# Starting each weight tile and each wide result tile at its own place modulo 128 bytes

## The chip, the core and the metric

The kernel runs on one core of a Trainium2 chip. The metric is the device time of one execution in microseconds; the median of three runs is compared. The profile comes from one more execution, taken by the hardware profiler.

## What is computed

The kernel does a linear recurrence with a complex decay over 768 steps for 4 x 8 heads of 48, and then a layer of 8 experts with two chosen per token. The change touches the experts alone:

```python
    logits = x @ w_gate
    noise_scale = np.log1p(np.exp(x @ w_noise))
    noisy_logits = logits + noise_scale * noise
    top2 = np.argpartition(-noisy_logits, 2, axis=1)[:, :2]
...
    for e in range(E):
        for k in range(2):
            mask = top2[:, k] == e
            h = np.maximum(x[mask] @ w1[e], 0.0)
            out[mask] += top2_w[mask, k, None] * (h @ w2[e])
```

Here E = 8, w1 is 384 x 1024 and w2 1024 x 384 for each expert, top2_w is a softmax over the two chosen, all is fp32 and there are 3072 tokens.

## The kernel before

**Stages.** In the first 260 us or so the recurrence runs in chunks of 128 steps; its gates, the choice of experts and the sending of rows to per-expert slots in DRAM run along with it, and the first weights are loaded. From there on the experts are worked one after the other. The order on each engine is written out by hand in two tables (EMIT and ORDER), and the change leaves both alone.

**An expert's slots.** Expert e (by rank) has a narrow part (w = 0) of 256 + REST[e] slots, with REST = 64, 64, 64, 48, 32, 16, 16, 0, and a wide part (w = 1) of 512 slots. So the narrow widths are 320, 320, 320, 304, 288, 272, 272 and 256.

**Split operands.** Each fp32 operand is kept as a rounded high part and a low rest. For the weights these are two tiles (`split`: a cast on ScalarE, ACT, and a subtraction on VectorE, DVE), named w1h and w1l for each of three blocks kk of 128 rows and two sets in turn (`w1{x}{kk}{e % 2}`), w2h and w2l for each of four. For x and h the high and the low part lie side by side in one tile.

**First products** (`mm1`, L896). For each of 8 blocks f of 128 columns, 9 matmuls accumulate into one PSUM tile `ph`: for kk = 0, 1, 2 the pairs (w1h, x high), (w1h, x low), (w1l, x high). A block of w1, 128 x 128, is the stationary operand (loaded by LDWEIGHTS), and x, 128 x width, moves. ACT writes the high part of h with a ReLU (L898), VectorE the low part (L901), into the tile `h{w}{f}`.

**Second products** (`mm2`, L922). For each tile j of 128 slots, 24 matmuls accumulate: for each f the pairs (h high, w2h), (h high, w2l), (h low, w2h). Here h is the stationary operand, 128 columns of it, and w2, 128 x 384, moves. The last slots of the narrow part, fewer than 128, take another form (L927, L930).

**Where tiles lie.** `mt` takes a tile from the pool that is open when its name is first used, and a pool places its tiles one behind the other in SBUF. Before the change the small tiles `spare`, `space0` and `space1`, which nothing reads, set the start: every tile of w1, w2, x and h starts 64 bytes past a multiple of 128 in each partition. A matmul's block starts a multiple of 512 bytes into its w1 tile, and so does a block of the high part of h. The low part of a wide h starts 2048 bytes into its tile, so it keeps the 64 bytes too. The low part of a narrow h starts behind the high part and its padding: for experts 3, 5 and 6 that is on a multiple of 128, for the others it is 64 past one.

Of the kernel before, what the change touches and what calls it, by code (L numbers as in the profile page):

```python
# [9 lines left out]
F32 = mybir.dt.float32  # L10
# [309 lines left out]
def kernel(  # L320
# [19 lines left out]
    ROW = 400  # L340
# [29 lines left out]
    cp = ctx.enter_context(tc.tile_pool(name="cp", bufs=1))  # L370
# [40 lines left out]
    nc.gpsimd.memset(none, 0.0)  # L411
    nc.gpsimd.memset(none[:, RNO:RNO + 1], float(NONE))
    xga = cp.tile([128, 3, ROW], F32, name="xga")
    cp.tile([128, ROW - 64], F32, name="spare")
    nc.gpsimd.memset(xga, 0.0)
    car = cp.tile([128, HD], F32, name="car")
    ncnt = small[:, 4:6]
# [329 lines left out]
    def rank():  # L747
        n = E - 2
        t = mt([128, 128], F32, name="order")
        key, place, which = t[:, 0:E], t[:, 8:8 + n], t[:, 16:16 + n].bitcast(I32)  # L750
        big, ONE[0] = (t[:, i:i + n * n].rearrange("p (r e) -> p r e", r=n) for i in (24, 64))
        ONE[2] = t[:, 100:100 + 4 * n].rearrange("p (j e) -> p j e", e=n)
        nc.vector.scalar_tensor_tensor(key, iota8, -(N + 1.0 / E), base_run, op0=OP.mult, op1=OP.add)
        nc.vector.tensor_tensor(big, key[:, None, 2:E].to_broadcast([128, n, n]),
                                key[:, 2:E, None].to_broadcast([128, n, n]), op=OP.is_gt)
        nc.vector.tensor_reduce(place, big, axis=AX.X, op=OP.add)
        nc.vector.tensor_tensor(ONE[0], iota8[:, 0:n, None].to_broadcast([128, n, n]),
                                place[:, None, :].to_broadcast([128, n, n]), op=OP.is_equal)
        nc.vector.tensor_mul(big, ONE[0], iota8[:, None, 2:E].to_broadcast([128, n, n]))
        with nc.allow_low_precision("whole numbers"):  # L760
            nc.vector.tensor_reduce(which, big, axis=AX.X, op=OP.add)
        ONE[1] = which
# [5 lines left out]
    def of(a, e):  # L768
        return a[e] if e < 2 else a[bass.ds(EX[e], 1)].rearrange("o a b -> (o a) b")
# [19 lines left out]
    def x_P(e, w):  # L789
        js = JS[w]  # L790
        src_t = (xga, xgb)[w]
        t = mt([128, len(js), 2, DM], U16, name=f"xp{w}")
        for i in range(len(js)):
            nc.scalar.copy(t[:, i], src_t[:, i, 0:DM].bitcast(U16).rearrange("p (d two) -> p two d", two=2))
        nc.sync.dma_start(xp[e % 2, js[0] * 128:(js[-1] + 1) * 128].rearrange("(j p) r -> p j r", p=128),
                          t.rearrange("p j two d -> p j (two d)"))

    def x_L(e, w):
        lo, n = JS[w][0] * 128, width(e, w)
        for kk in range(KD):  # L800
            x = XU[w, kk] = mt([128, 2, width(0, w)], U16, name=f"xu{w}", bufs=KD)[:, :, 0:n]
            for i in range(2):
                nc.sync.dma_start(x[:, i, :], xp[e % 2, lo:lo + n, i * DM + kk * 128:i * DM + (kk + 1) * 128], transpose=True)

    mctx = ctx.enter_context(ExitStack())
    mpools, psB = [], []
# [4 lines left out]

    W1, W2, XW, HT, GW, OX = {}, {}, {}, {}, {}, {}
    where = {}

    def mt(shape, dt, name, **kw):

        return where.setdefault(name, mpools[-1]).tile(shape, dt, name=name, **kw)

    def ps_tile(name, bufs=2):
        if psB:  # L820
# [7 lines left out]
    def split(raw_t, hi, lo):  # L828
        nc.scalar.copy(hi, raw_t)  # L829
        nc.vector.tensor_tensor(lo, raw_t, hi.bitcast(F32), op=OP.subtract)  # L830

    def load_w1(e):
        if e == 0:
            mt([128, 48], F32, name="space0")
        for kk in range(KD):
            r = mt([128, FF], F32, name="raw", bufs=RAW)
            nc.sync.dma_start(r, of(w1, e)[kk * 128:(kk + 1) * 128, :])
            W1[e, kk] = [mt([128, FF], F32R, name=f"w1{x}{kk}{e % 2}") for x in "hl"]
            split(r, *W1[e, kk])

    def load_w2(e):
        for f2 in range(KF // 2):
            r = mt([128, FF], F32, name="raw", bufs=RAW)
            rv = r[:, :2 * DM].rearrange("p (f d) -> p f d", f=2)
            nc.sync.dma_start(rv, of(w2, e)[f2 * 256:(f2 + 1) * 256, :].rearrange("(f p) d -> p f d", p=128))
            W2[f2] = [mt([128, 2, DM], F32R, name=f"w2{x}{f2}") for x in "hl"]
            split(rv, *W2[f2])
# [100 lines left out]
    for g in range(NG):  # L948
        f = B * g + .5
# [11 lines left out]
        for j in range(B):  # L961
            n = B * g + j
# [55 lines left out]

    at(NT - B + .5 - P["p3"] + 3 * P["d3"] + .01, close_f)
    at(P["w1"] + .5, load_w1, 0)  # L1020
    at(NT - .5 - P["q"] + .01, close_q)
    at(P["xt"] + .5, x_G, 0, 0)
# [3 lines left out]
    at(P["xt"] + .51, load_x, 1, 0, xga)  # L1026
    at(P["xu1"] + .5, x_G, 1, 0)
    at(P["w1b"] + .5, load_w1, 1)
    at(P["w2"] + .5, load_w2, 0)
    for f in range(KF):  # L1030
# [89 lines left out]
    halves(mm1, 0, 1, then)  # L1120
    then(load_x, 1, 1, xgb)
    then(load_w1, 2)
    halves(mm2, 0, 1, then)
    x_in(1, 1, then)
# [263 lines left out]
```

## Time and profile before

| | |
|---|---|
| median of three runs | 677.25 us (675.72 to 677.81) |
| profiled execution, its own time | 679.66 us |
| profiled execution, first to last instruction | 677.9 us |
| PE (matmuls) busy | 656.7 us |
| VectorE, ScalarE busy | 434.5 us, 357.6 us |
| chain that ended last: L896, L922 | 29% and 28% of the span |

PE is TensorE's matmuls and PEld its weight loads, which overlap them. A matmul's duration in the rows is longer than the distance between two starts, since matmuls are pipelined; the distance is what adds up.

### The profile page before, as it was taken

How to read it: one execution, taken by the hardware profiler on the slowest of the kernel's cores; microseconds unless marked ns; L12 is line 12 of the kernel's file. 1: busy time of each engine (PE TensorE's matmuls, PEld its weight loads, DVE VectorE, ACT ScalarE, POOL GpSimd, SP SyncE). 2: the span in 40 equal slices, each digit the busy share in tenths (PEclk: the TensorE clock that was granted, in tenths of full speed). 3: DMA queues.
4: the chain of work that ended last, by engine and by line, in shares of the span. 5: the costliest groups of instructions: out<-in, count | busy, mean ns of one | idle time of the engine just before them, and what ended most of it. 6: DMA issues, size and time to landing. Idle time of an engine off the chain costs nothing.

```text
span 677.9 us, 14399 instructions
## 1 busy us (share of the span) xinstructions
PE 656.7 (97%) x5519; PEld 578.1 (85%) x5519; DVE 434.5 (64%) x998; ACT 357.6 (53%) x596; POOL 173.3 (26%) x209
## 2 busy tenths in 40 slices
PE   7999999999989999999999999999999999999995
PEld 3477787878878899899998999999899899899895
DVE  7999999999978667444456367248337437527311
ACT  7899999999755552344226227118217406404300
POOL 3000000344443331033324124124231422422211
PEclk9999999999999999999999999999999999999998
DMA  6757667758487635256718447827636646842201
GB/s 239 232 177 193 195 156 247 219 179 273 148 244 263 216 116 203 73 174 181 220 65 299 130 140 278 149 105 272 159 122 243 164 134 218 194 127 72 63 36 35
DMA packets 100220, 117.85 MB, mean 174 GB/s; under 512 B 57338, under 2 KB 79307, under 8 KB 100144
## 3 DMA queue, kind: packets, MB, share of 16 engines
q1 hardware_dynamic: 90816, 89.32, 43.7%
q0 software_dynamic: 9328, 27.54, 12.7%
q8 instruction: 45, 0.74, 0.4%
q14 instruction: 31, 0.25, 0.1%
HBM read 70.26 MB, written 40.02 MB: 163 GB/s over the span
## 4 chain that ended last, share of the span: by engine, by line
PE 76%; DVE 8%; ACT 3%; DMA 2%; issue 1%; another core or an unknown queue 1%; SPq 0%; POOL 0%; POOLq 0%
PE ph L896 29%; PE po L922 28%; PE ptr L577 3%; PE psc L587 2%; PE pY L636 2%; PE pY L638 2%; PE psc L896 2%; PE po L930 1%; PE po L927 1%; PE cum L646 1%; DVE am L588 1%; PE cum L554 1%; DMA out_dram<-none 1%; DVE w1l L830 1%; PE cum L527 1%
## 5 line engine op out<-in xcount | busy, mean ns | idle before, releaser
L922 PE MATMUL po<-w2h,h 128*128 128x384 f32 x768 | 198.6, 335 | 0.0
L896 PE MATMUL ph<-x,w1h 128*128 128x512 f32 (+5 forms) x720 | 186.6, 347 | 0.0
L922 PEld LDWEIGHTS po<-w2h,h 128*128 128x128 f32 x768 | 139.0, 188 | 1.0 <-DVE h L901 0.3
L896 PEld LDWEIGHTS ph<-x,w1h 128*128 128x128 f32 x720 | 125.6, 188 | 15.1 <-DVE x L881 0.4
L922 PE MATMUL po<-w2l,h 128*128 128x384 f32 x384 | 128.4, 334 | 0.0
L896 PE MATMUL ph<-x,w1l 128*128 128x512 f32 (+5 forms) x360 | 124.8, 347 | 0.2 <-DVE w1l L830 0.2
L901 DVE SCALAR_TENSOR_TENSOR h<-ph,h 128x512 fp32r<-128x512 f32 (+5 forms) x168 | 71.1, 456 | 80.1 <-ACT h L898 72.5
L936 POOL DMA_INDIRECT out_dram<-ao,ox x55 | 58.1, 1056 | 247.8 <-DVE ao L935 210.5
L898 ACT ACTIVATE h<-ph 128x512 fp32r<-128x512 f32 (+5 forms) x120 | 61.1, 515 | 98.7 <-PE ph L896 85.3
L711 POOL DMA_INDIRECT xs<-xr,sl x48 | 52.8, 1100 | 186.2 <-DVE im L506 119.7
L935 DVE SCALAR_TENSOR_TENSOR ao<-po,gw,ao 128x384 f32<-128x384 f32 (+4 forms) x55 | 33.7, 613 | 78.3 <-PE po L922 77.2
L896 PEld LDWEIGHTS ph<-x,w1l 128*128 128x128 f32 x360 | 67.7, 188 | 8.1 <-DVE w1l L830 0.5
L922 PEld LDWEIGHTS po<-w2l,h 128*128 128x128 f32 x384 | 72.1, 188 | 0.4
L907 POOL DMA_INDIRECT ao<-out_dram,ox x48 | 53.3, 1111 | 51.7 <-issue 41.2
L880 ACT CAST x<-xj 128x512 fp32r<-128x512 f32 (+5 forms) x36 | 18.9, 524 | 63.6 <-DVE xj L877 63.6
L587 PEld LDWEIGHTS psc<-qT,kT 112*64 112x64 f32 x768 | 36.4, 137 | 6.7 <-issue 2.8
L587 PE MATMUL psc<-qT,kT 112*64 112x128 f32 (+1 forms) x768 | 40.2, 250 | 1.7 <-DVE h L901 1.4
L638 PE MATMUL pY<-am,v 128*48 128x128 f32 x384 | 36.4, 273 | 0.7 <-issue 0.4
L830 DVE TENSOR_TENSOR w2l<-raw,w2h 128x768 fp32r<-128x768 f32 x32 | 30.2, 953 | 8.1 <-ACT w2h L829 8.0
L588 DVE TENSOR_TENSOR am<-psc,mask 128x512 f32<-128x512 f32 x48 | 32.6, 684 | 3.6 <-PE psc L587 2.9
L829 ACT CAST w2h<-raw 128x768 fp32r<-128x768 f32 x32 | 26.3, 834 | 15.2 <-PE po L922 8.7
L636 PE MATMUL pY<-qT,z 112*48 112x128 f32 x320 | 31.8, 275 | 0.0
(229 smaller groups left out, 998.7 us busy)
## 6 DMA issues: line engine op xcount, KB each, us to landing
raw<-in_moe_w_dram SPq DMA_DIRECT2D x24, 512.0 KB
raw<-in_moe_w_dram SPq DMA_DIRECT2D x32, 384.0 KB
qk<-in_qk_dram SPq DMA_DIRECT2D x24, 384.0 KB
v<-in_v_dram SPq DMA_DIRECT2D x24, 288.0 KB
xgb<-xs SPq DMA_DIRECT2D x8, 800.0 KB
re<-in_a_dram SPq DMA_DIRECT2D x12, 384.0 KB
im<-in_a_dram SPq DMA_DIRECT2D x12, 384.0 KB
out_dram<-none SPq DMA_DIRECT2D x12, 384.0 KB
```

Of the source, the lines that this page charges most:

```text
L587: nc.tensor.matmul(p[o:o + 64, j, z:], KT[n][:, h, z:z + 64], QT[n][:, h, z:], start=True, stop=True, skip_group_check=True)
L588: nc.vector.tensor_mul(AM[n][:, 4 * half:4 * half + 4, :].rearrange("p (a r) t -> p a (r t)", r=2), p.rearrange("p (a r) t -> p a (r t)", ...
L636: nc.tensor.matmul(o, Z[b][:, h, :], QT[n][:, h, :], start=True, stop=False, skip_group_check=True)
L638: nc.tensor.matmul(o, V[n][:, H + h // 2 if h % 2 else h, :], AM[n][:, h, :], start=not g, stop=True, skip_group_check=True)
L711: d = nc.gpsimd.indirect_dma_start(out=xs, out_offset=bass.IndirectOffsetOnAxis(ap=sl[:, kk, b:b + 1], axis=0), in_=XR[g][:, lo + b, :], i ...
L830: nc.vector.tensor_tensor(lo, raw_t, hi.bitcast(F32), op=OP.subtract)
L896: nc.tensor.matmul(p[:, :n], W1[e, kk][i][:, f * 128:(f + 1) * 128], XW[w, kk][:, j, :], start=(c == 0), stop=(c == len(ms) - 1))
L898: nc.scalar.activation(h[:, 0:n], p[:, :n], AF.Relu)
L901: nc.vector.scalar_tensor_tensor(h[:, dst:dst + b - a], p[:, a:b], 0.0, h[:, a:b].bitcast(F32), op0=OP.max, op1=OP.subtract)
L907: nc.gpsimd.indirect_dma_start(out=ao[j][0:w, :], out_offset=None, in_=out, in_offset=bass.IndirectOffsetOnAxis(ap=OX[e][0:w, j:j + 1], ax ...
L922: nc.tensor.matmul(p[:, :DM], HT[w, f][i][:, o:o + 128], W2[f // 2][k2][:, f % 2, :], start=(m == 0), stop=(m == len(ms) - 1))
L936: d = nc.gpsimd.indirect_dma_start(out=out, out_offset=bass.IndirectOffsetOnAxis(ap=OX[e][0:n, j:j + 1], axis=0), in_=a, in_offset=None, b ...
```

## The change

The tiles of w1 and of the wide h (h10 to h17) get starts of their own. `AT` gives for a name an offset in bytes; the tile is taken 8 columns (32 bytes) longer, and the view that the kernel uses begins that offset into it. Since each tile is 32 bytes longer, the next one starts 32 bytes further modulo 128, and the offset is added to that. Two small tiles `space2` and `space3` behind the w1 tiles put what follows back to 64, and `spare` gives up 768 bytes, 6 x 128, to make room.

```diff
-    cp.tile([128, ROW - 64], F32, name="spare")
+    cp.tile([128, 144], F32, name="spare")
...
+    AT = dict(w1h00=4, w1l00=8, w1h10=16, w1l10=12, w1h20=8, w1l20=16, w1h01=12, w1l01=12, w1h11=24, w1l11=28,
+              w1h21=16, w1l21=28, h10=4, h11=16, h12=8, h13=28, h14=8, h15=0, h16=0)
...
-        return where.setdefault(name, mpools[-1]).tile(shape, dt, name=name, **kw)
+        o, n = AT.get(name, -1) // 4, shape[-1]
+        t = where.setdefault(name, mpools[-1]).tile(shape if o < 0 else [128, n + 8], dt, name=name, **kw)
+        return t if o < 0 else t[:, o:o + n]
...
+        if e < 2:
+            mt([128, 16], F32, name=f"space{e + 2}")
```

Starts of the views modulo 128 bytes, from the places that the built programs give their tiles:

| tiles, in the order of use | before | after |
|---|---|---|
| w1h, w1l of kk = 0, 1, 2, first set | 64 each | 68, 104; 16, 44; 72, 112 |
| w1h, w1l of kk = 0, 1, 2, second set | 64 each | 76, 108; 24, 60; 80, 124 |
| wide h, f = 0 to 7, both parts | 64 each | 68, 112, 8, 60, 72, 96, 0, 32 |
| x, w2, narrow h (high part) | 64 each | 64 each |
| tiles of the row exchange behind the wide h (xp, xu, xj) | 64 each | 32 each |

In columns of 4 bytes, and modulo 32 of them, a step from one w1 tile to the next is 9, 10, 7, 7, 10, 21 in the first set and 8, 11, 9, 5, 11, 20 in the second; from one wide h to the next it is 11, 6, 13, 3, 6, 8, 8, 9.

No instruction is added, removed or moved on any engine. Since tiles lie over other tiles of the pools that were closed before, a few waits move; on ACT, around the first cast of w2h, a row before reads

```order
287 L829 CAST w2h_3714<-raw 128x768 [waits DMAHW4_49]
288 L639 ACTIVATE xT<-pY 128x512
289 L461 ACTIVATE ga1w_3232<-ga1e 128x1 [waits DVE_49]
290 L647 COPY xr<-cum 128x384 [waits PE_49]
291 L578 ACTIVATE kT<-ptr 112x1024 [waits PE_49]
```

and in the changed kernel (on ACT, too)

```order
287 L832 CAST w2h_3715<-raw 128x768 [waits DMAHW4_49,DVE_49]
288 L639 ACTIVATE xT<-pY 128x512
289 L461 ACTIVATE ga1w_3233<-ga1e 128x1
290 L647 COPY xr<-cum 128x384 [waits PE_49]
291 L578 ACTIVATE kT<-ptr 112x1024 [waits PE_49]
```

The cast now waits for VectorE as well as for its load, and the activation behind it, which waited for VectorE, no longer has to. Further on, a wait for one load goes from the copy `lo` to the next cast of x.

## Rows read from the trace of the kernel before

**Rows 1.** The page's head and the clock slices (40 equal ones)

```profile
span 677.9 us, 14399 instructions
PE 656.7 (97%) x5519; PEld 578.1 (85%) x5519; DVE 434.5 (64%) x998; ACT 357.6 (53%) x596; POOL 173.3 (26%) x209
PEclk9999999999999999999999999999999999999998
```

**Rows 2.** The chain in order of time: start us, length us, engine, line, count

```profile
260.90 8.33 PE ph L896 x55
...
329.18 2.08 PE ph L896 x9
...
350.70 5.27 PE ph L896 x36
...
603.66 16.64 PE po L922 x96
...
670.30 0.63 DVE ao L935
```

**Rows 3.** Narrow first products: chain in short windows; two timeline rows of 304 columns

```profile
406.93 7.16 PE ph L896 x52
407.74 0.30 PE L896 MATMUL ph<-x,w1h 128*128 128x304 f32 x1
407.87 0.30 PE L896 MATMUL ph<-x,w1l 128*128 128x304 f32 x1
460.45 7.64 PE ph L896 x58
513.89 7.19 PE ph L896 x57
620.30 7.79 PE ph L896 x65
```

**Rows 4.** Wide first products of expert 4: the chain in a short window

```profile
469.90 14.75 PE ph L896 x65
```

**Rows 5.** Second products of expert 3, narrow (432 us), wide (443 us): chain, timeline of PE

```profile
432.38 8.38 PE po L922 x48
...
433.08 0.52 PE L922 MATMUL po<-w2h,h 128*128 128x384 f32 x2
...
433.62 0.50 PE L922 MATMUL po<-w2h,h 128*128 128x384 f32 x2
...
434.13 0.51 PE L922 MATMUL po<-w2h,h 128*128 128x384 f32 x2
...
443.73 0.52 PE L922 MATMUL po<-w2h,h 128*128 128x384 f32 x2
...
444.26 0.51 PE L922 MATMUL po<-w2h,h 128*128 128x384 f32 x2
...
444.78 0.51 PE L922 MATMUL po<-w2h,h 128*128 128x384 f32 x2
```

**Rows 6.** Timeline of ACT and VectorE around the first cast of w2h

```profile
218.56 0.95 DVE L567 TENSOR_TENSOR kh<-qk,tr 128x768 f32<-128x768 f32 x1
220.19 0.82 ACT L829 CAST w2h<-raw 128x768 fp32r<-128x768 f32 x1
```

**Rows 7.** Groups by form: busy us, mean ns of one | idle before, releaser

```profile
L896 PEld LDWEIGHTS ph<-x,w1h 128*128 128x128 f32 x720 | 125.6, 188 | 15.1 <-DVE x L881 0.4 <-DVE h L901 0.2
L901 DVE SCALAR_TENSOR_TENSOR h<-ph,h 128x512 fp32r<-128x512 f32 x64 | 43.3, 690 | 65.7 <-ACT h L898 59.5 <-issue 6.2
L898 ACT ACTIVATE h<-ph 128x512 fp32r<-128x512 f32 x64 | 38.1, 603 | 73.3 <-PE ph L896 60.7 <-PE po L922 6.6 <-issue 5.9
```

## The prediction

> **What bounds the kernel now.** I read the page's head first, then the chain of waits in order of time, then the chain again in short windows, and last the timeline of TensorE (PE). The head [rows 1] gives a span of 677.9 us with PE busy for 97% of it and the granted clock at its upper level, 2.4 GHz, in nearly all slices. The chain [rows 2] is one engine from 260.90 us to 670.30 us: blocks of L896 (first products) and of L922 (second products) follow each other without a gap, and only the tail behind 670.30 us belongs to others. So from 260.90 us on, the time is the sum of PE's matmul spacings, and nothing else there is late. The change moves no instruction of any engine (told below), so the question is what one matmul costs when its weights start elsewhere.
>
> A matmul over N columns at 2.4 GHz needs N/2.4 ns. What it takes beyond that I call its excess, and I get it from the chain in windows: piece length over count, less N/2.4. In the narrow first products of experts 3, 4, 5 and 7 [rows 3] the widths are 304, 288, 272 and 256 (256 + REST; two timeline rows show the first). 7.16 us/52 = 137.7 ns, less 126.7, is 11.0 ns at 304. 7.64/58 = 131.7 less 120.0 is 11.7 at 288. 7.19/57 = 126.1 less 113.3 is 12.8 at 272. 7.79/65 = 119.8 less 106.7 is 13.2 at 256. In the wide ones [rows 4] 14.75/65 = 226.9 less 213.3 is 13.6 at 512. Expert 1's narrow ones, 320 wide, give 5.27/36 = 146.4 less 133.3, 13.1 [rows 2]. The second products have N = 384 and give 16.64/96 = 173.3 less 160.0, 13.3 [rows 2].
>
> Two things are to be seen. First, 13.3 ns is 32 columns at 2.4 GHz, and 32 columns of fp32 are 128 bytes: the widths that are multiples of 64 sit at that value, and the three that are not (304, 288, 272) sit below it. Second, in the kernel before every weight tile and every h tile starts 64 bytes past a multiple of 128, with one exception: the lower halves (h's second half) in the narrow groups of experts 3, 5 and 6, which the padding puts on a multiple of 128. The second products that read those [rows 5] take 8.38 us/48 = 174.6 ns, an excess of 14.6, and their timeline steps unevenly: a period of three matmuls lasts from 0.51 us (433.62 to 434.13) to 0.54 us (433.08 to 433.62), where the same loop with all starts alike repeats at 0.52 to 0.53 us. The program is the same there; only the place of the stationary operand differs. So the place of the weights does act on PE's spacing, and with starts alike it settles at 32 columns.
>
> A rule speaks against that. The Trainium skill, "TensorE: Matmul & The Clock Gate", Part 2, step 1, says that PE has two independent SBUF read ports and that loading the next weights takes nothing from the running matmul; its back-to-back gap is N/2.4 + 2.5 ns. The trace disagrees on the size (13.3 against 2.5) and, in rows 5, on the independence. By that rule the change would do nothing and the time would stay 677.2 us.
>
> **The change part by part.** (1) What moves. Instruction order is the same on all five engines. Two waits change place on ACT: the first cast of w2h now also waits for VectorE, and a wait of a copy goes to a later cast. The cast starts at 220.19 us and the last VectorE work ahead of it that reads a tile of that older pool, kh, ends at 218.56 + 0.95 = 219.51 us [rows 6], so it waits for nothing; behind it on ACT stand xT and ga1w, which would slip by the same amount if VectorE were later than 220.19 us. Cost: 0.
>
> (2) First products, 1152 matmuls (9 for each of 8 f, two widths, 8 experts). All of them load w1, whose six tiles now start at six different places, 5 to 21 columns apart from one weight to the next. Three of nine consecutive loads repeat a place, six step.
>
> (3) Second products of the wide part, 768 matmuls (24 for each of 4 tiles, 8 experts). They load h1, which now starts at eight places; three loads in a row share a place, then it steps by 3 to 13 columns.
>
> (4) Everything else on PE keeps its starts: x, w2, the narrow h. The second products of the narrow part keep their cost.
>
> No row shows these steps, so I bound them. The nearest rows are those in which PE does not settle. Below: 11.0 ns (304 wide, the stretch that never settles); below that, the shortest single spacing in that stretch is 0.13 us (407.74 to 407.87), 130 ns or 3.3 over [rows 3]; no stretch holds it, so the floor that I use is halfway, 7 ns. Above: 14.6 (mixed starts, rows 5), and for wide matmuls 2.08 us/9 = 231.1, 17.8, in the nine that follow a switch from other work [rows 2].
>
> I take 11.0 ns for all that sat settled. The reason is that the new starts differ by steps that are no multiple of 16 columns. That resembles 304, where a matmul ends half a period off and the next start falls at a new phase, more than it resembles rows 5, where the starts differ by exactly 64 bytes. Wide first products: 576 x (13.6 - 11.0) = 1.50 us. Second products: 768 x (13.3 - 11.0) = 1.77 us. Narrow first products at 320 and 256 on the path (144 + 72): 216 x 2.1 = 0.45 us. Those at 304, 288 and 272 are unsettled already and keep their mean. The sum is 3.7 us, all on the path, since nothing else is late between 260.90 and 670.30 us. What comes next if PE gets faster: ACT's h at 603 ns and VectorE's at 690 ns, 1.29 us for a wide f of 9 x 227 = 2.04 us [rows 7], and ACT waits for PE there (60.7 us in total), so they stay ahead. The same margin hides writes to odd places, if those are slower: it takes over 0.7 us more for each f until PE waits. The profiled execution took 679.66 us, 2.4 above the median of 677.25; the saving lies in matmuls that are the same in each run, so I subtract it from the median: 673.5 us.
>
> **The rivals.** *Slower through mixed starts.* Rows 5 are the only direct look at weights that start in different places, and they cost 1.3 ns more per matmul, not less. At that price 1560 matmuls (576 + 768 + 216) cost 2.0 us. If moreover the wide ones never get past what follows a switch (17.8), 576 x 4.2 = 2.4 us takes the place of their 0.75: 3.7 us, 680.9. I give it 680.0, between them and nearer the second, since a step in each triple is a switch over and over. It decides where the mean excess stays over 13.4 ns. For it: rows 5. Against it: 304, 288 and 272 are unsettled too and cheaper.
>
> *Slower through odd words.* Of the 20 moved tiles 13 start off a multiple of 16 bytes. Every weight row is 512 bytes; if it is read in pieces of 16, such a start makes 33 pieces of 32, 1/32 of the load's 188 ns [rows 7], 5.9 ns as an estimate. Loads last longer than the spacing, so the rows can't exclude that it shows. On 9 of 12 w1 tiles and 4 of 8 h1 tiles: 1152 x 0.75 x 5.9 + 768 x 0.5 x 5.9 = 7.4 us, 684.6. The Trainium skill states such a rule ("SBUF — State Buffer", Specifications: 16-byte cachelines, each crossing to a new line pays). No row here has an operand off 16 bytes, so nothing bears on it either way.
>
> *No difference.* The steps cancel within a cycle: a start that is moved up by 9 columns is paid back by the one that goes back 11. The starts of w1 and of h1 come back to where they began after each cycle, which speaks for it; that excess can be other than 32 columns on average (11.0 at 304) speaks against. Time: 677.2 us.
>
> *Much faster.* Every start falls where the next load can take it at once: 7 ns. 576 x 6.6 + 768 x 6.3 + 216 x 6.1 = 10.0 us, 667.3.
>
> **How the numbers follow.** Forecast (about 11 ns) 0.45, much faster 0.08, no difference 0.22, mixed starts 0.20, odd words 0.05. About 0.3% (2.0 us) is what a measurement of this kernel can tell from no change. Faster is 0.45 + 0.08 = 0.53, same 0.22, slower 0.25. The range has to leave out no more than 0.2: from 667.5 (half of the much faster case falls out) to 680.5 (the odd words and the upper third of the mixed starts fall out).
>
> **What would show it.** Right: in the chain of the changed kernel a block of 96 second products lasts 16.4 us instead of 16.64, and 65 wide first products last 14.58 instead of 14.75, with an uneven timeline. Wrong: blocks of 16.77 us or more (mixed starts), or of 16.64 with equal steps (the place doesn't matter). Odd words would show as a weight load longer than 188 ns on the odd tiles alone. If ACT or VectorE end a wait of PE behind 260.90 us, my cover for the writes is wrong.

## The result, and the profile after

The changed kernel takes 680.66 us (median of 4 runs, 679.87 to 681.29) against 677.51 us for the kernel before in the same comparison: a ratio of 1.0051, interval 1.003 to 1.0073. It is slower by 0.5%, where 0.6% faster was forecast.

The page's head and clock slices of the changed kernel, to be held against [rows 1]:

```profile
span 679.3 us, 14400 instructions
PE 659.6 (97%) x5519; PEld 579.7 (85%) x5519; DVE 434.8 (64%) x998; ACT 356.9 (53%) x596; POOL 174.3 (26%) x209
PEclk9999999999999999999999999999999999999998
```

PE's busy time is 2.9 us longer, its counts are the same, and the granted clock is the same row. The chain of the changed kernel, as in [rows 2], [rows 3] and [rows 5] (start us, length us, engine, line, count; L901 is L896 of before, L927 is L922):

```profile
257.05 8.34 PE ph L901 x55
...
330.94 16.83 PE po L927 x96
...
347.76 5.27 PE ph L901 x36
...
404.68 9.00 PE ph L901 x65
...
415.31 15.07 PE ph L901 x65
430.38 8.38 PE po L927 x48
...
469.32 15.41 PE ph L901 x66
...
621.73 7.72 PE ph L901 x65
...
671.37 0.63 DVE ao L940
```

With the same arithmetic as ahead of the result:

| matmuls | before | after |
|---|---|---|
| wide first products (512 columns), odd experts: 15.07/65 | 13.6 [rows 4] | 18.5 ns |
| wide first products, even experts: 15.41/66 | 13.6 [rows 4] | 20.2 ns |
| wide second products (384 columns): 16.83/96 | 13.3 [rows 2] | 15.3 ns |
| narrow second products, expert 3: 8.38/48 | 14.6 [rows 5] | 14.6 ns |
| narrow first products, 320 columns: 5.27/36 | 13.1 [rows 2] | 13.1 ns |
| 304 columns: 9.00/65 | 11.0 [rows 3] | 11.8 ns |
| 256 columns: 7.72/65 | 13.2 [rows 3] | 12.1 ns |

Nearly all that lost is wide. Over all eight experts, taken from the starts of single matmuls (distances that are more than 35 ns over N/2.4, nearly all of them switches and waits, left out), the wide first products go from 14.3 to 19.0 ns and the wide second ones from 13.4 to 15.4. Seven of the distances left out in the changed kernel are no switches: 42 or 43 ns, once or twice in each even expert, always at the same place of the same sequence. With them the wide first products are at 19.3. That is 2.8 and 1.5 us, 4.3 us together. Of the narrow first products those of 304 and 288 columns lose 0.7 and 1.2 ns, those of 272 stay the same on the mean, and those of 256 gain 1.1; all narrow ones together lose 0.1 us.

From the block of 55 first products to the last DVE piece the chain of before lasts from 260.90 to 670.30 us [rows 2], 409.4 us, and that of after from 257.05 to 671.37, 414.3 us: 4.9 us more. The spans differ by only 1.4 us, because the profiled execution of before holds, ahead of this stage, a piece that the chain of after has nothing like (chain of the kernel before):

```profile
200.09 3.81 another core or an unknown queue
```

So the two spans must not be subtracted from each other; the timed medians differ by 3.15 us (2.0 to 4.9 by the interval). A piece of 3.7 to 3.8 us like this one stands in five of the sixteen profiles, with starts alike and with starts unlike, so it is not the change's doing. The last run with the wide starts of before (rows 5 mended, below) has no such piece: its span is 675.3 us, 4.0 under the changed kernel's, and the same stretch lasts 409.4 us in it as in the kernel before.

What PE waited for from 257 to 670 us in the changed kernel (engine, line, waited for: us, times, longest), and its weight loads (ns min/median/max):

```profile
PE ph L901 <- DVE h L906: 0.3, 1, 0.3
PE ph L901 <- DVE w1l L833: 0.2, 1, 0.2
```

```profile
L901 PEld LDWEIGHTS ph<-x,w1h x720: 186/188/195, 255.3 to 645.3; 128*128 128x128 f32 x180
```

The wait for w1l is there before, too; the one for h is new and 0.3 us. Weight loads at the new places take the same 188 ns as in [rows 7]. No other engine took PE's place: the spacing itself grew.

### The profile page after: what moved, and what is told of

It is laid out like the page before. It is cut to its first block, busy times and chain, and to the rows that moved or that the text cites. A ratio compares the mean times of both kernels' runs of the same rounds, so it can differ in the third digit from the quotient of the medians.

```text
span 679.3 us, 14400 instructions
## 1 busy us (share of the span) xinstructions
PE 659.6 (97%) x5519; PEld 579.7 (85%) x5519; DVE 434.8 (64%) x998; ACT 356.9 (53%) x596; POOL 174.3 (26%) x209
## 3 DMA queue, kind: packets, MB, share of 16 engines
q0 software_dynamic: 9328, 27.54, 12.5%
## 4 chain that ended last, share of the span: by engine, by line
PE 71%; DVE 10%; ACT 4%; DMA 3%; issue 2%; SPq 0%; POOL 0%; POOLq 0%; DVEq 0%; ACTq 0%
PE ph L901 28%; PE po L927 28%; PE ptr L577 2%; PE psc L587 2%; PE psc L901 2%; PE pY L636 2%; PE pY L638 1%; PE po L935 1%; PE po L932 1%; DVE am L588 1%; DMA xgb<-xs 1%; PE cum L646 1%; DMA out_dram<-none 1%; DVE im L522 1%; ACT L460 1%
## 5 line engine op out<-in xcount | busy, mean ns | idle before, releaser
L927 PE MATMUL po<-w2h,h 128*128 128x384 f32 x768 | 199.8, 337 | 0.0
L901 PE MATMUL ph<-x,w1h 128*128 128x512 f32 (+5 forms) x720 | 188.8, 350 | 0.3 <-DVE h L906 0.3
L927 PEld LDWEIGHTS po<-w2h,h 128*128 128x128 f32 x768 | 139.5, 188 | 1.1 <-DVE h L906 0.3
L901 PEld LDWEIGHTS ph<-x,w1h 128*128 128x128 f32 x720 | 125.9, 188 | 17.0 <-issue 0.5
L927 PE MATMUL po<-w2l,h 128*128 128x384 f32 x384 | 129.2, 336 | 0.0
L901 PE MATMUL ph<-x,w1l 128*128 128x512 f32 (+5 forms) x360 | 125.5, 349 | 0.2 <-DVE w1l L833 0.2
L901 PEld LDWEIGHTS ph<-x,w1l 128*128 128x128 f32 x360 | 67.7, 188 | 9.0 <-DVE w1l L833 0.5
L927 PEld LDWEIGHTS po<-w2l,h 128*128 128x128 f32 x384 | 72.1, 188 | 0.4
L885 ACT CAST x<-xj 128x512 fp32r<-128x512 f32 (+5 forms) x36 | 18.9, 524 | 64.5 <-DVE xj L882 64.5
L832 ACT CAST w2h<-raw 128x768 fp32r<-128x768 f32 x32 | 26.4, 835 | 15.2 <-PE po L927 8.7
L833 DVE TENSOR_TENSOR w1l<-raw,w1h 128x1024 fp32r<-128x1024 f32 x24 | 29.2, 1221 | 4.4 <-ACT w1h L832 4.4
```

What stands on the lines that cost most here:

```text
L901: nc.tensor.matmul(p[:, :n], W1[e, kk][i][:, f * 128:(f + 1) * 128], XW[w, kk][:, j, :], start=(c == 0), stop=(c == len(ms) - 1))
L927: nc.tensor.matmul(p[:, :DM], HT[w, f][i][:, o:o + 128], W2[f // 2][k2][:, f % 2, :], start=(m == 0), stop=(m == len(ms) - 1))
```

## The experiments

In all tables the numbers are the mean excess in ns (distance of two starts less N/2.4), taken from the starts in the trace as above, with distances over 35 ns left out (where that leaves out some that belong to the sequence, the text says so). Places are columns of 4 bytes modulo 32 in the first two maps, modulo 64 (256 bytes) later; 16 is the place of the kernel before. Times are compared with those of the kernel before on the same chip, which differ from chip to chip (676.1 to 681.3 us).

### One half of the change at a time

Two runs: the changed kernel with the offsets of h taken out of `AT` (the edit shown), and the changed kernel with those of w1 and the two spaces taken out:

```diff
-              w1h21=16, w1l21=28, h10=4, h11=16, h12=8, h13=28, h14=8, h15=0, h16=0)
+              w1h21=16, w1l21=28)
```

> Only the w1 tiles begin at places of their own; the wide h tiles stay 64 bytes past a multiple of 128. Mixed starts: the wide first products (512 columns) go from 14.3 ns over N/2.4 to 18.5 to 19.5, which over 576 matmuls is 2.4 to 3.0 us; the wide second products stay at 13.3 to 13.5 (a block of 96 lasts 16.64 us). Time 2.0 to 3.0 us over the kernel before. No effect of the w1 starts (the whole loss is in h): wide first products within 0.3 ns of 14.3, time within 0.5 us of the kernel before.

> Only the wide h tiles begin at places of their own; every w1 tile stays 64 bytes past a multiple of 128. Mixed starts: the wide second products (384 columns) take 15.0 to 15.8 ns over N/2.4 instead of 13.4, which over 768 matmuls is 1.2 to 1.8 us (a block of 96 lasts 16.80 to 16.87 us instead of 16.64); the wide first products stay at 14.3. Time 1.0 to 2.0 us over the kernel before, and with the run that moves w1 alone this adds up to the changed kernel's loss. If the two parts only act together: both single runs within 0.5 us of the kernel before.

Measured: w1 alone 679.19 us against 676.13 before, ratio 1.005 (1.0033 to 1.0066); h alone 676.93, ratio 1.0016 (1.0003 to 1.0028). Chains of w1 alone (experts 3 and 4, wide first, then wide second products):

```profile
415.16 14.84 PE ph L901 x64
...
468.77 15.41 PE ph L901 x66
...
495.30 16.64 PE po L927 x96
```

and of h alone (expert 4, the same two):

```profile
467.36 14.97 PE ph L898 x66
...
493.45 16.82 PE po L924 x96
```

With w1 moved, 14.84/64 and 15.41/66 are 18.5 and 20.2 ns over, and the second products stay at 16.64. With h moved, the first products settle (14.97/66 is 13.5 over) and the second take 16.82. The halves act on their own matmuls alone. 3.06 and 0.8 us add up to 3.9, within the interval of the whole. The spacings came out as expected; of the times, 3.06 lies at the upper end of its range, and 0.8 (0.2 to 1.9) a little under the 1.0 that was expected at least.

### Maps: a pattern for each expert

Every tile of w1 and of the wide h is lengthened, and an offset that depends on the expert picks the start:

```diff
+            for i in (2 * kk, 2 * kk + 1):
+                o = (PW[e][i] - 16 - 24 * i) % 32
+                W1[e, kk].append(mt([128, FF + 24], F32R, name=f"w1{'hl'[i % 2]}{kk}{e % 2}")[:, o:o + FF])
...
+                o = (PH[e][f] - 16) % 32
+                h = mt([128, 2 * n + 32], F32R, name=f"h{w}{f}")[:, o:o + 2 * n]
```

> Each expert has its own starts (columns of 4 bytes modulo 32). w1 in the order h, l of kk 0, 1, 2: expert 2 all at 0; 3: 16, 0 in turn; 4: up by 8; 5: the changed kernel's first set rounded to multiples of 4; 6: the changed kernel's first set; 7: down by 8. Wide h, f = 0 to 7: expert 2 all at 17; 3: 16, 0 in turn; 4: up by 4; 5: down by 4; 6: the changed kernel's; 7: the same rounded to multiples of 4. Experts 0 and 1 keep 16. Odd words: the 17 of expert 2 costs 2 to 6 ns more per second product, and rounding to multiples of 4 brings 18 to 19 ns back to 14.3 (first products) and 15.4 back to 13.4 (second). Mixed starts: all at 0 and all at 17 stay at 14.3 (512 columns) and 13.3 (384 columns), rounding changes nothing (18 to 19.5 and 15 to 15.8), and every pattern with steps is dearer than 14.3 and 13.3; the direction of the steps, up or down, may matter.

> As the map before, with other starts. w1: expert 2 up by 4 from 4; 3: up by 1 from 22; 4: up by 2 from 20; 5: 16, 16, 0, 0, 16, 16; 6: down by 4 from 16; 7: the changed kernel's second set. Wide h: expert 2 all at 0; 3: up by 1 from 16; 4: up by 8; 5: up by 2; 6: up by 12; 7: down by 1. Mixed starts, whatever the step: all patterns with steps lie at 15 to 20 ns for the first products and 14.5 to 16 for the second. If the size of the step decides: steps of 1 and 2 columns stay within 1 ns of 14.3 and 13.3, and the cost grows with 4, 8 and 12. If the direction decides: steps up by small amounts give less than 13.3, steps down more, or the other way round. Expert 2's second products (all at 0) stay at 13.3 in each.

| w1 starts (wide first products) | ns | h starts (wide second products) | ns |
|---|---|---|---|
| all 16 (experts 0 and 1, first map) | 19.1, 18.9 | all 16 (experts 0 and 1, first map) | 15.6, 16.7 |
| all 0 | 18.8 | all 17 | 15.6 |
| 16, 0 in turn | 18.7 | 16, 0 in turn | 15.6 |
| up by 8; down by 8 | 19.2; 18.5 | up by 4; down by 4 | 15.2; 15.7 |
| changed kernel's first set | 19.6 | changed kernel's | 15.3 |
| the same, rounded to multiples of 4 | 18.5 | the same, rounded | 15.2 |
| up by 4; by 1; by 2; down by 4 | 17.7; 19.4; 17.8; 18.7 | up by 1; 2; 8; 12; down by 1 | 15.0; 15.8; 14.4; 14.8; 14.8 |
| changed kernel's second set; 16, 16, 0, 0, 16, 16 | 21.3; 20.4 | all 0 | 13.3 |

Both expectations missed on one point, and that point taught most. Experts 0 and 1 have all starts at 16, as before, and should have stayed at 14.3 and 13.4. They did not, and neither did all at 0 (w1) and all at 17 (h) in the first map (expert 1's second products there):

```profile
331.42 16.97 PE po L934 x96
```

16.97/96 is 16.8 over. Alike modulo 128 bytes is not enough: the lengthening makes each tile begin an odd number of 128 bytes behind the one before it (with one exception among the six of w1), so the starts take turns between two places modulo 256. The distances there repeat after six matmuls, that is after two f, which is what a period of 256 bytes gives:

```
17   8  18  25  16  16  17   8  18  25  16  16   (ns over 160, expert 1, first map)
```

These turns of 128 bytes lie under every pattern of both maps. Rounding to 16 bytes changes nothing. That alone doesn't rule out the odd words, since the turns by themselves cost about as much (15.6 to 16.7 and 18.9 to 19.1); the runs without steps below do. Chain of the first map, second products with the changed kernel's h starts (expert 6) and with the same rounded (expert 7):

```profile
604.56 16.82 PE po L934 x96
...
654.74 16.82 PE po L934 x96
```

The first products lie at 17.7 or more for every pattern, up or down, small steps or large (up by 1 is at 20.7 if four distances over 35 ns, which recur in it, are counted).

### All starts moved together

```diff
-    cp.tile([128, ROW - 64], F32, name="spare")
+    cp.tile([128, ROW - 80], F32, name="spare")
```

> The kernel before with its filler tile 64 bytes shorter: w1, w2, x and h all begin on a multiple of 256 bytes, where before all begin 64 bytes past one. Theory that only differences between starts matter: first products (512 columns) stay at 14.3 ns over N/2.4, second (384 columns) at 13.4, and the time stays within 1 us of the kernel before. Theory that the 64 bytes matter by themselves: both move by over 1 ns, the time by over 2 us.

680.88 us against 680.24, ratio 1.0018 (0.9999 to 1.0037); 14.2 and 13.4 ns. The 64 bytes by themselves cost nothing that can be seen.

### Modulo 256, and one place for h against w2

The maps again, but the wide h and five of the six w1 tiles of the even experts are 64 columns (256 bytes) longer and the offsets are taken modulo 64; w1 of the odd experts is as before.

> Here tiles are lengthened by 256 bytes, so that starts differ by nothing modulo 256 but by what is set; steps of 256 between neighbours remain. Wide h, all eight f at one place, in columns of 4 bytes modulo 64, experts 0 to 7: 16 (as w2), 17, 20, 24, 0, 32, 48, 8. If starts that are alike modulo 256 settle wherever they are, all eight experts take 13.3 to 13.8 ns over N/2.4 in the second products; if the place of h against that of w2 matters, expert 0 takes 13.3 and others differ by over 0.5; if the modulus is larger than 256 bytes, expert 0 takes over 14.5 too. w1 of the even experts, h and l of kk 0, 1, 2: expert 0 all at 16 (14.3 if the modulus is 256 at most); 2: the last one at 48; 4: 16, 32, 48, 0, 16, 32; 6: up by 1 from 16 (18 to 20 each if any step costs).

> As the map before with other starts, in columns modulo 64. Wide h: experts 0 to 3 take two places 32 apart in turn, from 0, 8, 16 and 24; experts 4 to 7 go up by 16, 48, 24 and 40. In the maps before, two places 128 bytes apart gave 13.3 from 0 and 15.6 to 16.7 from 16; if the place against w2 is what differs, 0 gives about 13.3 again, 16 over 15.5, 8 and 24 lie between; if only the step counts, all four are alike. w1 of the even experts: 0: 16, 48 in turn; 2: 16, 24 in turn; 4: 16, 16, 48, 48, 16, 16; 6: 16, 20 in turn: 17.5 to 20.5 ns each by the theory that any mixture keeps the first products from settling, under 15 for the one whose step is free.

Expert 0, whose tiles now stand 4096 + 256 bytes apart, has 14.4 and 13.7: steps of 256 bytes cost nothing. Chain of the first of these two maps: expert 2's wide first products (last w1 tile 128 bytes off), expert 3's (nothing off), expert 5's second products (all h at 32):

```profile
364.74 14.84 PE ph L908 x65
...
418.33 14.74 PE ph L908 x65
...
551.41 16.96 PE po L934 x96
```

One tile of six that is off costs 15.1 ns on the mean of its expert. The ladders are at 18.2 and 18.6, and in the other map 16, 48 in turn gives 18.0; 16, 24 gives 19.7; 16, 20 gives 18.9; pairs give 18.2. None is free.

A surprise is in the second products. All eight f at one place give 13.3 to 13.4 at 20, 24 and 0, 13.7 at 16, but 16.6 at 17 and 32, 16.0 at 48 and 16.7 at 8, with w2 at 16. So likeness among the weights is not enough: the distance to the moving operand acts as well. Nor is likeness always needed: two places 32 columns apart give 13.3 from 0, but 15.4 from 8, 14.4 from 16, 15.9 from 24.

### Distance without steps

```diff
+                h = mt([128, 2 * n + 64], F32R, name=f"h{w}{f}")[:, o:o + 2 * n]
...
+            x = mt([128, 2 * n + 64], F32R, name=f"x{w}{kk}")[:, PX[e]:PX[e] + 2 * n]
```

> No steps at all: modulo 256 bytes all weights of a stretch begin at one place and all moving operands at one place, but the two places differ, by another distance for each expert. Wide h against w2, experts 0 to 7, in columns of 4 bytes: +2, +3, +6, +12, +20, +24, +36, +44. Wide x against w1: 1, 2, 4, 8, 16, 24, 32, 48. Theory that only steps between weights cost: 14.3 ns over N/2.4 for the first products, 13.4 for the second, at every distance. Theory that the distance between the two operands sets which spacing they settle at: 13.3 or 16.7 (32 or 40 columns) by expert, as in the map with distances of 0, 1, 4, 8, -16, 16, 32 and -8; a distance that settles under 12 would be a faster kernel.

> As the run before with other distances. Wide h against w2: +5, +10, +20, +28, -20 (44), -15 (49), -8 (56), -1 (63). Wide x against w1: 3, 6, 12, 20, 40, 56, 60, 63. Steps only: 14.3 and 13.4 throughout. Distance: 13.3 or 16.7 by expert; the -8 and the +20 that occur twice give what they gave before if the distance alone decides, and may give the other value if what came ahead of the stretch decides.

In the first of these the last four distances of h were in fact 36, 40, 52 and 60 columns. Measured, with the run before:

| second products, h against w2 | ns |
|---|---|
| 0, 2, 4, 5, 8, 12, 28, 44, 48, 49 | 13.3 to 13.7 |
| 1, 3, 6, 16, 32, 36, 40, 52, 60, 63 | 15.6 to 17.3 |
| 10; 20 | 19.8; 16.0 |
| 56 (-8), in two runs | 16.7; 13.3 |

First products, x against w1: 15.6 at 3, 15.7 at 16, 16.7 at 12, and 17.8 to 24.8 at the thirteen others (24.8 at a distance of one column); 14.3 where the distance is 0. The "steps only" theory falls. But it is not the distance alone either: 56 gives both values. Chains at 56 columns (expert 7 of the first map modulo 256), at 56 again and at 49 (experts 6 and 5 of the second run here):

```profile
655.52 16.96 PE po L934 x96
...
603.76 16.64 PE po L932 x96
...
549.09 16.64 PE po L932 x96
```

The first repeats 18 15 20 14 (mean 16.7), the second 11 15 12 15 (mean 13.3): two steady sequences at one distance. What the stretch comes out of may decide between them; no run tests it. None gave a mean under 13.2.

These runs also settle the odd words. With h 2, 5 or 49 columns from w2 every block of h starts 4 or 8 bytes off a multiple of 16, and the second products take 13.3 to 13.7; at 16, 32, 36, 40, 52 and 60 columns h starts on such a multiple, and they take 15.6 to 17.3.

### One step

> One weight tile steps aside, all others begin alike modulo 256 bytes. Wide h: f = 7 alone is off by 1, 2, 4, 8, 16, 24, 32, 48 columns in experts 0 to 7, one step there and one back in 24 second products. w1 of the even experts: the last of the six tiles alone is off, by 4, 16, 1 and 8 columns in experts 0, 2, 4 and 6, one step there and back in 9 first products; 32 columns cost 14 ns in each 9 in an earlier run. Price for each step, whatever its size: 12 to 18 ns in each 9 for all four, so 15.0 to 15.7 ns on the mean, and some 12 ns in each 24 for all eight h, 13.9. Price that grows with the size: 1 and 2 columns under 0.3 ns on the mean, 32 most. By the forecast's view (steps let the next start fall where it can be taken at once): under 13.3.

Means of the first products: 14.4 with the last w1 tile off by 4 columns, 15.8 by 16, 16.3 by 1, 15.8 by 8; the second products 13.9 to 14.7 with one f off. Nothing is under 13.3, and no order by size: for the first products 4 columns cost nothing, 1 column costs most. The single distances, nine first products in a row (ns over 213.3), show what a step does:

```
14 14 13 14 14 13 14 14 13   all alike, settled
13 14 14 13 14 14 13 14 14   last tile off by 4 columns
20 17 14 14 13 14 14 22 15   last tile off by 8 columns
11 25 17 23 19 19 19 19 17   changed kernel, expert 3
```

One tile off by 8 throws the sequence out (22 15), the way back does it again (20 17), and then it settles: 22 + 15 + 20 + 17 less 4 times 13.3 is 21 ns for two steps. In the changed kernel the next step comes before it has settled.

Steps cost by themselves, not only through the distance that comes with them: one f of h that is 2, 8 or 48 columns off gives 14.4, 14.4 and 14.2, while all eight f at these distances gave 13.3 to 13.7. And the distance alone doesn't price a step: x 60 columns from w1 gave 23.2 for all six tiles, while the last tile alone at that distance (off by 4) costs nothing. In the changed kernel both are at work, and no run tells their shares apart.

### The steps out again, and the fix for rows 5

> The tiles lie elsewhere and apart (wide h and five of the six w1 tiles of the even experts are 256 bytes longer), but all views begin 64 bytes past a multiple of 256 again, so the steps are out while the moving of tiles and the lengthening stay. If steps modulo 256 bytes are the cause: first products (512 columns) 14.1 to 14.5 ns over N/2.4, second (384 columns) 13.3 to 13.6, time within 1 us of the kernel before. If the moving of the tiles as such costs (other neighbours in memory, the place of the engines' writes): 680 us or a like loss of 2 us or more against the kernel before in the same call.

Chain, expert 4's wide first and second products:

```profile
473.09 14.96 PE ph L908 x66
...
499.16 16.64 PE po L934 x96
```

14.96/66 is 13.3, 16.64/96 is 13.3; 681.39 us against 681.33, ratio 0.9995 (0.9974 to 1.0015). Lengthened and displaced tiles cost nothing while their starts are alike modulo 256 and equal to those of the moving operand.

```diff
-            HT[w, f] = h[:, 0:m + t], h[:, m + t:]
+            lo = -(-(m + t) // 64) * 64
+            HT[w, f] = h[:, 0:m + t], h[:, lo:]
```

> The kernel before, but the low half of a narrow h begins at a multiple of 64 columns of its tile, so that experts 3, 5 and 6, whose low halves began on a multiple of 256 bytes where the high ones are 64 past one, have all starts alike. If likeness modulo 256 is what counts: their narrow second products go from 14.6 ns over N/2.4 to 13.8 to 14.0, as in experts 4 and 7, which over 144 matmuls is 0.1 us; the time can't tell that from no change (within 1 us). If not: 14.6 stays.

Narrow second products of experts 3 and 4:

```profile
429.22 8.35 PE po L923 x48
...
482.82 8.34 PE po L923 x48
```

By single starts experts 3, 5 and 6 go from 14.6 to 13.9, as experts 4 and 7. The sequence of [rows 5] has the same cause, the place of the low half. The gain of 0.1 us can't be seen in the time (ratio 0.9999, 0.9977 to 1.0022).

### Why 512 columns pay most

The same w1 starts cost about 5 ns at 512 columns and next to nothing at 256 to 320.

```diff
-                nc.tensor.matmul(p[:, :n], W1[e, kk][i][:, f * 128:(f + 1) * 128], XW[w, kk][:, j, :],
+                v = (512, 512, 512, 448, 416, 384, 352, 320)[e] if w and c else n
+                nc.tensor.matmul(p[:, :v], W1[e, kk][i][:, f * 128:(f + 1) * 128], XW[w, kk][:, j, 0:v],
```

> The changed kernel, but in the wide first products eight of nine matmuls take fewer columns of x: 512, 448, 416, 384, 352, 320 in experts 2 to 7 (the products of the columns left out are missing from the result). w1 starts as changed. If the number of columns sets what unsettled starts cost: about 19 ns over N/2.4 at 512, 15 to 16 at 384, 12.5 to 13.5 at 320, the rest between. If the place of the wide x or the wide part as such sets it: 18 to 19.5 at each width. If a step costs a fixed 7 to 9 ns: 18 to 19 at each width too.

> The same widths with the starts of the kernel before, all alike (the products of the columns left out are missing from the result here too). 13.3 to 14.3 ns over N/2.4 at 512, 448, 384 and 320 if widths that are multiples of 64 settle; 416 and 352, odd multiples of 32, don't settle and give 10.5 to 12.5 as 288 does, if it is the remainder by 64 that keeps 288 from settling; 13.3 there too if a multiple of 32 is enough.

Chain with the changed kernel's starts, five f of experts 2, 3, 4 and 7:

```profile
363.31 10.48 PE ph L902 x45
...
416.99 9.33 PE ph L902 x45
...
469.26 8.77 PE ph L902 x45
...
619.63 7.20 PE ph L902 x46
```

Of nine matmuls one has 512 columns and eight have 512, 448, 416 and 320; less their columns at 2.4 GHz this is 19.6, 17.7, 17.1 and 14.3 ns. Of the seven of each nine that begin and end beside narrow ones, the means are 20.5 (distances of 43 ns counted; 19.6 without them), 17.6, 16.9, 15.3 (384), 14.0 (352) and 14.1. At 320, 12.5 to 13.5 was expected. The price falls with the columns, in the wide part's own place in memory, so neither that place nor a fixed price for a step sets it.

The control missed its expectation. With all starts alike (experts 3 and 7):

```profile
416.30 9.61 PE ph L897 x46
...
618.42 7.03 PE ph L897 x45
```

9.61/46 less 189.6 is 19.3 at 448, 7.03/45 less 142.2 is 14.0 at 320; by the seven of nine 18.8, 15.8, 15.1, 14.1, 13.7 for 448 to 320. One matmul of another length in nine, it seems, keeps the sequence from settling just as unlike starts do, so this run is no clean control. It says that unsettled costs much the same at a given width whatever unsettles it (within 1.2 ns from 320 to 448), and that 448 columns cost more than 13.3 though all starts are alike.

## Why the prediction was wrong

*What bounds the kernel* held. The time is the sum of PE's spacings, no wait took over but one of 0.3 us, the granted clock is the same, and the moved wait on ACT cost nothing that shows. VectorE's and ACT's cover held too.

*That the place of the stationary operand acts on the spacing*, read from [rows 5], held, and [rows 5] itself yields to the low half's alignment: 14.6 to 13.9, so 0.7 of the 1.3 ns that were read there belong to the starts. Its measure was too small, 256 bytes and not 128, and likeness is not all of it, since the distance to the moving operand acts too.

*The step that failed* is "I take 11.0 ns for all that sat settled". It carried the value of the 304-wide row [rows 3] to 384 and 512 columns, by a likeness of phases. That gave the wrong sign:

| term | forecast | measured |
|---|---|---|
| wide first products, 576 | -1.50 us | +2.8 us (14.3 to 19.3 ns) |
| wide second products, 768 | -1.77 us | +1.5 us (13.4 to 15.4 ns) |
| narrow first products at 320 and 256 | -0.45 us | -0.04 us (-0.08 at 256, +0.04 at 320) |
| narrow first products at 304, 288 and 272 | 0 | +0.1 us |
| sum | -3.7 us | +4.4 us in the traces, +3.15 in the medians |

What the runs showed in its place: unsettled spacing depends on the columns. With the changed kernel's starts it is 12 to 13 ns at 256 to 304, 13 to 14 at 320 and 352, 15 at 384, 17 to 18 at 416 and 448, 18.6 to 20.1 at 512, while settled is 13.1 to 13.7 at each of 256, 320, 384 and 512. At 256 columns unsettled is cheaper than settled, at 320 about even, from 384 on dearer. The 11.0 at 304 was a true price of the wrong width. The two rows at the right widths were in the prediction, as bounds: 14.6 at 384 [rows 5], measured 15.4, and 17.8 at 512 behind a switch [rows 2], measured 18.5 and 20.2.

*The rivals.* "Slower through mixed starts" is what happened, in direction and nearly in size (680.0 named, 680.66 measured), and its sign is in the chain: a block of 96 second products lasts 16.83 us, where 16.77 or more was named. Its better half was the clause that the wide first products never get past what follows a switch: in the changed kernel the next step comes before the sequence of the last one has run out ("One step"). Its 1.3 ns was too little for the second products (2.0) and too much for the narrow first ones at 320 and 256 (0.2 and -1.1). "Odd words" falls: h at starts off 16 bytes takes 13.3 to 13.7 where the distance suits, and loads stay at 188 ns. (Its premise that loads last longer than the spacing holds at 384 columns, 188 against 173 ns, and not at 512, with 227.) "No difference" falls: coming back to the first place after each cycle does not pay back: a way there and back by 8 columns cost 21 ns. "Much faster" falls: in all the distances and patterns nothing at 384 or 512 columns had a mean under 13.2.

On the rule of the Trainium skill, "TensorE: Matmul & The Clock Gate", Part 2, step 1, that loading weights takes nothing from the running matmul: by that the change does nothing. The traces disagree, since instructions, durations of the loads and clock are the same and the spacing goes from 13.3 to 15.3 at 384 columns, and from 13.6 to 18.5 and 20.2 at 512, with the place alone. The N/2.4 + 2.5 ns that the prediction sets beside the 13.3 is given there for an isolated matmul (the Trainium skill, same page, "Back-to-back issue gap"); every matmul here has a weight load of its own, so no run bears on that figure. On the rule of the Trainium skill, "SBUF — State Buffer", Specifications, that each crossing to a new 16-byte line pays: no run here shows a price for starts off such lines (13.3 to 13.7 at 2, 5 and 49 columns).

One row is named wrongly in the prediction: 5.27/36 [rows 2] belongs to expert 2, not expert 1. Its width, 320, is the same, and so is the sum.

*What stays open:* which resource makes a matmul wait when starts differ, why that wait grows with the columns, and how the changed kernel's loss divides between the steps and the distance to the moving operand. The runs show the condition and the price, not the circuit.

## What to carry to other kernels

Where PE is the bound and matmuls follow each other with a new stationary operand each, start from one rule: give all the stationary tiles that follow each other the same start modulo 256 bytes, the moving operand that start too (or another distance that has been measured), and keep their strides multiples of 256; halves inside a tile count too. It is shown here for fp32 blocks of 128 x 128 alone. When a price for an unsettled state is taken from a row, take it from a row of the same width: the row nearest in kind was here worth less than the row nearest in size.

## What the runs showed that was not expected

- The period is 256 bytes: 64 columns of fp32. Tiles 4096 + 128 bytes apart (one pair of six 4096) cost 18.9 to 19.1 ns at 512 columns, tiles 4096 + 256 apart 14.4. Yet second products whose h takes turns of 128 bytes from place 0 have a mean of 13.3.
- Without any step, the distance between the stationary and the moving operand alone moves the second products between 13.3 and 19.8 ns and the first between 14.3 and 24.8. At the same distance (56 columns) both 16.7 and 13.3 occurred, each as a steady sequence.
- A settled sequence comes back: four matmuls after a step there and back by 8 columns, five to eleven after a switch from other work, and with the same distances each time.
- Steps of 4 columns can be free (one tile off, 14.4 ns) and dear (in turn, 18.9).
